# Token sums in two halves: reciprocals, stores and broadcasts of a recurrent attention loop

## The chip, the cores and the metric

The kernel runs on one core of one Trainium2 chip. The metric is the device time of one execution in microseconds. The reference is a plain array program; the kernel has to give its output from the same inputs in one launch. In the text PE is the matrix engine, DVE the vector engine, ACT the scalar engine, POOL the general engine, and SP the engine that issues nearly all transfers.

## The reference

Two branches read the same 2048 tokens of 512 channels and are mixed by a gate. The branch with the recurrence is what matters here:

```python
mem = mem0                                    # 8 rows of 512
for s in range(n_seg):                        # 64 segments of 32 tokens
    h = concatenate([mem, x[32 tokens]])      # 40 rows
    q, k, v = h @ Wq, h @ Wk, h @ Wv          # 32 heads of 128
    scores = where(mask, q @ k.T * scale, -1e9)
    o = softmax(scores) @ v
    o = einsum('bhte,hed->btd', o, Wo)
    mem = o[:, :8]                            # goes into the next segment
    outs.append(o[:, 8:])
out = g * concatenate(outs) + (1 - g) * mlp(layernorm(x))
```

The mask lets every row see the memory rows and lets a token see itself and what lies before it. A segment can't begin before the memory rows of the segment before it are there.

## The kernel before, in words

First comes the channel MLP of all tokens, from which a gated part `c` of the output goes to DRAM (`c_dr`) while the weights of the attention are loaded. After that a loop runs over the 64 segments; `T` is the tile of 128 tokens, `si` one of its four segments. The order of the instructions on every engine is written out by hand; the instructions of an engine, and the transfers that SP issues, run in the order of the program.

In a segment, 24 of the 32 tokens and the 8 memory rows are handled as one group of 32 rows; the 8 tokens that are left over in each of four segments ("left") are handled together for a whole tile. Work for the next tile's left rows (`side`) is put between the steps of a segment. The steps of a segment, in the order of PE:

- Q and K of the rows (`qk_unit`, line 124), copied by ACT (line 129) and transposed by DVE (line 133).
- Scores of the first sixteen heads into PSUM bank `SbF`, exponentials into `E` by ACT (line 751); V (line 143); then scores of the other sixteen into bank `W` (lines 294 and 298) and their exponentials (line 740).
- Sums over the keys. They are of two kinds. For the 8 memory rows `msum` gives the sums, and `mnorm` takes their reciprocal (line 747) and multiplies it into `E` (line 748), so these rows are normalized before the product with V. For the 32 tokens `xsums` (line 645) gives the sums of a half, 4 columns of `xs8`; the products with V are made with unnormalized `E`, and are normalized later.
- `recip_x` after the second half: one reciprocal of 8 columns (line 656), a store of it to DRAM (`r_dr`, line 659), and a load of it that is broadcast to all 128 partitions (`Rb`, 512 KB, line 660). The load waits until the store has landed.
- E V (`av`, lines 318 and 323), memory rows copied to `UT` (line 784), token rows to `XR` (line 651).
- The output pass (`wo_pass`, line 155) over `UT`, with the memory rows of this segment beside the tokens of the segment before; its memory rows go into the next segment through `new_mem` (lines 688 and 690).

The normalization of the tokens, `x_norm` on POOL (line 672), stands at the head of the next segment: `XR` times `Rb` into `UT` and `UL`. So a segment's tokens pass through the output pass of the segment after it. POOL also adds up the reciprocals (`racc`, line 664) and DVE keeps their minimum (`rmin`, line 804): at the end a flag is made from them, and if they are out of bounds a slow general version is run.

For all tiles but the last two, the outputs of the pass are four partial sums in partitions, which are brought together by DRAM: `put_w` (line 243) stores the output of a segment to `w_dr`, `get_w` (line 252) loads its four parts side by side into `G`, `put_left` (line 246) and `get_left` (four loads, line 256) do the same for the left rows, and `add_parts` (lines 261 to 269) adds them on DVE and stores the output. In the loop, before the change, these four stand at the head of a segment:

```python
        if s >= 2 and s - 2 < SPT * (NT - 2):
            put_w(s - 2, ws.pop(s - 2))
        if 4 <= s < SPT * (NT - 2) + 4:
            get_w(s - 4)
        if si == 3 and 1 <= T < NT - 1:
            put_left(T - 1)
        if si == 0 and T >= 2:
            get_left(T - 2)
```

Of the kernel before, what the change touches and what calls it, by code (L numbers as in the profile page):

```python
# [21 lines left out]
R_MIN = 1.0e-30  # L22
RSUM_MAX = 1.0e25
# [4 lines left out]
def kernel(ctx, tc, A_x, A_mem0, A_Wq, A_Wk, A_Wv, A_Wo, A_seg_len, B_x, B_w1, B_b1, B_w2, B_b2, gate_w, out):  # L28
    nc = tc.nc
    P = 128  # L30
# [210 lines left out]
    def put_w(s, w):  # L241
        T, si = divmod(s, SPT)
        nc.sync.dma_start(w_dr[T % 2][si], w[:])

    def put_left(T):
        nc.sync.dma_start(l_dr[T % 2][:], wls.pop(T)[:])

    def get_w(s):
        T, si = divmod(s, SPT)
        if si == 0:  # L250
            Gs[T] = cw.tile([P, 4, Dm], BF16, tag="G", name="G")
        nc.sync.dma_start(Gs[T][seg * si:seg * si + RIDE], w_dr[T % 2][si].rearrange("(c r) e -> r c e", c=4)[M:32])
# [76 lines left out]
    with tc.tile_pool(name="mlpw", bufs=1) as mlpw, \  # L329
# [44 lines left out]
        m0 = ep.tile([M, Dm], BF16)  # L374

        def loads(blk):
            if 2 * blk + 7 < NT:
# [270 lines left out]
    def x_raw(s):  # L648
# [2 lines left out]
            nc.scalar.copy(out=XR[:, j], in_=U[j][:, 0:NG * 40].rearrange("p (i q) -> p i q", q=40)[:, :, 0:32])  # L651
        XRs[s] = XR

    def recip_x(s):
        R = Rs.pop(s)
        nc.vector.reciprocal(out=R[:, 8 * NG:RW], in_=xs8)

        Rb = cw.tile([P, P, NG], FP32, tag="Rb", bufs=1, name="Rb")
        nc.sync.dma_start(r_dr[s % 2][:], R[:, 8 * NG:RW])
        nc.sync.dma_start(Rb[:].rearrange("p r e -> p (r e)"), r_dr[s % 2][:].rearrange("r e -> (r e)").partition_broadcast(P))  # L660
        for i2 in (1, 0):
            nc.vector.tensor_copy(out=R[:, 32 * i2:32 * i2 + 32], in_=RP[i2])
        mask_put(0)
        nc.gpsimd.tensor_tensor(out=racc[:, 0:RW], in0=racc[:, 0:RW], in1=R[:, 0:RW], op=ALU.add)  # L664
        Rbs[s] = Rb

    def x_norm(s):
        T, si = divmod(s, SPT)
        XR, Rb = XRs.pop(s), Rbs.pop(s)[:].rearrange("p (c q) (h j) -> p h j c q", c=4, h=2)
        for out, o, a, b in ((UT[(s + 1) % 2], M, LEFT, 32), (UL[T % 2], LEFT * si, 0, LEFT)):  # L670
            for h in range(2):
                nc.gpsimd.tensor_tensor(out=out[:, :, 4 * h:4 * h + 4, o:o + b - a], in0=XR[:, :, 4 * h:4 * h + 4, a:b], in1=Rb[:, h, :, :, a:b], op=ALU.mult)  # L672

    def wo_pass(U_, cuts=(0, Dm)):
        for n in range(NW):
# [18 lines left out]
    for s in range(nseg):  # L694
        T, si = divmod(s, SPT)
        last = s == nseg - 1
        hc, hn = hT[s % 3], hT[(s + 1) % 3]
        fill = side(T, si)
        if s + 1 < nseg:
            prep_h(s + 1)  # L700
        if s >= 1:
            x_norm(s - 1)
        if si == 0 and T >= 2:
            c_load(T - 2)
        if si < 3:
# [6 lines left out]
        if s >= 2 and s - 2 < SPT * (NT - 2):  # L712
            put_w(s - 2, ws.pop(s - 2))
        if 4 <= s < SPT * (NT - 2) + 4:
            get_w(s - 4)
        if si == 3 and 1 <= T < NT - 1:
            put_left(T - 1)
        if si == 0 and T >= 2:
            get_left(T - 2)
# [12 lines left out]
        V = cw.tile([P, NG, Dh], BF16, tag="V", name="V")  # L732
        E = cw.tile([P, NG, EW], BF16, tag="E", name="E")
        R = cw.tile([P, NG * 40], FP32, tag="R", name="R")
        Rs[s] = R
        xsum = SbF[:, 0:32 * NG].rearrange("p (i q) -> p i q", q=32)

        def exps(i2, x):
            c = slice(0, 40) if x else slice(40, EW)
            nc.scalar.activation(out=E[:, 4 * i2:4 * i2 + 4, c], in_=Sb[i2][:, :, c], func=ACTF.Exp, scale=scale)  # L740

        def msum(i2):
            sums(U[i2][:, 320:352].rearrange("p (i q) -> p i q", q=8), E[:, 4 * i2:4 * i2 + 4, :], 40, 48, 8, True)

        def mnorm(i2):
            r, e = RP[i2], E[:, 4 * i2:4 * i2 + 4, 40:56].rearrange("p i (a q) -> p i a q", q=8)
            nc.vector.reciprocal(out=r, in_=U[i2][:, 320:352])
            nc.vector.tensor_tensor(out=e, in0=e, in1=r.rearrange("p (i q) -> p i q", q=8).unsqueeze(2).to_broadcast([P, 4, 2, 8]), op=ALU.mult)

        scores(s, 0)  # L750
        nc.scalar.activation(out=E[:, 0:4, :], in_=Sb[0], func=ACTF.Exp, scale=scale)
        for kc in range(KC):
            v_unit(X1, hc, 0, kc)

        def v_cast(vb, h):
            i0 = 4 * vb + 2 * h
            nc.scalar.copy(out=V[:, i0:i0 + 2, :].rearrange("p i e -> p (i e)"), in_=(X1, X2)[vb][:, 256 * h:256 * h + 256])  # L757
# [48 lines left out]


    nx = slice(8 * NG, 40 * NG)
    sums(xsum, E, 8, 0, 32, True)
# [5 lines left out]
    nc.vector.reciprocal(out=R[:, nx], in_=SbF[:, 0:32 * NG])  # L815
    ws[s - 1] = wo_pass(UT[s % 2])
    Rr = R[:, nx].rearrange("p (i q) -> p i q", q=32)
# [7 lines left out]
    for _ in fill:  # L825
        pass
    flush(act_q, 9)
    nc.vector.tensor_tensor(out=rmin[:, nx], in0=rmin[:, nx], in1=R[:, nx], op=ALU.min)
    nc.vector.tensor_tensor(out=racc[:, nx], in0=racc[:, nx], in1=R[:, nx], op=ALU.add)
    okp = loop.enter_context(tc.tile_pool(name="okp", bufs=1))  # L830
    tot = okp.tile([P, 2], FP32)
    nc.vector.tensor_reduce(out=tot[:, 0:1], in_=rmin[:], axis=AX.X, op=ALU.min)
    nc.vector.tensor_reduce(out=tot[:, 1:2], in_=racc[:], axis=AX.X, op=ALU.add)
    good = okp.tile([P, 2], BF16)
    nc.vector.tensor_scalar(out=good[:, 0:1], in0=tot[:, 0:1], scalar1=R_MIN, scalar2=None, op0=ALU.is_gt)
    nc.vector.tensor_scalar(out=good[:, 1:2], in0=tot[:, 1:2], scalar1=RSUM_MAX, scalar2=None, op0=ALU.is_lt)
    wf = wo_pass(UF, (0, Dm // 2, Dm))

    wl, c = wls.pop(T), cs.pop(T)
# [140 lines left out]
```

## Time and profile before

| | us |
|---|---|
| median of 3 runs | 771.27 (769.58 to 772.21) |
| profiled execution | 773.18 |
| its span, first to last instruction | 771.4 |
| PE busy | 751.8 |
| ACT busy | 538.7 |
| DVE busy | 428.2 |
| POOL busy | 303.4 |

The mean granted clock of PE was 0.996. The profiled execution's own time is 1.8 us over its span, and 1.9 us over the median of the runs. An instruction group's row gives the line, the engine, the operation, what it writes and reads, the count, the busy time, the mean of one, and the idle time of the engine before it with what ended most of it. A timeline row gives start and duration in us from the span's start. Idle time of an engine that isn't the bottleneck costs nothing by itself.

### The profile page before, as it was taken

Reading aid. Unit: us, or ns where it says so; the run is one execution under the profiler, and the core shown is the slowest. Engines: PE = TensorE matmul, PEld = TensorE weight load, DVE = VectorE, ACT = ScalarE, POOL = GpSimd, SP = SyncE. Lnnn points to the kernel's source line nnn. Section 1 sums busy time; section 2 is a strip of 40 time slices with the busy share of each in tenths; the row PEclk is TensorE's granted clock in tenths of the full one; section 3 lists DMA queues with packets and bytes.
Section 4 is the critical chain, followed back from the end, with each engine's and each line's share of the span. In section 5 each row is a group of like instructions: output and inputs, shape, how many; then the busy total and the mean of one; then the engine's idle time right before and its main releaser. Section 6 shows DMA issues by size and latency. Waiting matters only on the chain.

```text
span 771.4 us, 43914 instructions
## 1 busy us (share of the span) xinstructions
PE 751.8 (97%) x19074; PEld 409.3 (53%) x19074; DVE 428.2 (56%) x1470; ACT 538.7 (70%) x1631; POOL 303.4 (39%) x522
## 2 busy tenths in 40 slices
PE   7999999999999999999999999999999999999996
PEld 5666555555455555555555555554555555555453
DVE  5776355544546455555646464645554564646454
ACT  4666677777677677777776777776777777777663
POOL 4111034342544443444435254544434443543441
PEclk9999999999999999999999999999999999999999
DMA  6779422323233433414333332332331333332312
GB/s 196 274 237 391 154 64 70 99 93 112 86 85 89 115 98 95 114 60 114 99 113 99 103 104 85 94 111 89 100 112 63 109 99 113 99 106 75 88 42 66
DMA packets 71688, 87.11 MB, mean 113 GB/s; under 512 B 23545, under 2 KB 61410, under 8 KB 69954
## 3 DMA queue, kind: packets, MB, share of 16 engines
q1 hardware_dynamic: 69762, 81.36, 34.0%
q8 instruction: 151, 2.47, 1.4%
q0 software_dynamic: 784, 1.97, 0.8%
q10 hardware_dynamic: 944, 0.92, 0.4%
q14 instruction: 47, 0.39, 0.2%
HBM read 64.30 MB, written 13.63 MB: 101 GB/s over the span
## 4 chain that ended last, share of the span: by engine, by line
PE 94%; DMA 2%; issue 1%; DVE 1%; ACT 1%; POOL 1%; DVEq 0%; POOLq 0%; SPq 0%; ACTq 0%
PE U L124 29%; PE X L143 18%; PE W L155 15%; PE X L124 7%; PE U L503 5%; PE U L318 4%; PE X L155 4%; PE SbF L497 2%; PE W L497 2%; PE U L305 1%; PE W L294 1%; PE U L688 1%; PE SbF L294 1%; PE SbF L645 1%; DMA b1r<-in_B_b_dram 1%
## 5 line engine op out<-in xcount | busy, mean ns | idle before, releaser
L672 POOL TENSOR_TENSOR UT<-XR,Rb 128x384 bf16<-128x384 bf16 x126 | 139.8, 1132 | 307.5 <-DMA Rb<-r_dr 254.8
L129 ACT CAST Tb<-U 128x512 bf16<-128x512 f32 x258 | 151.2, 586 | 80.2 <-PE U L124 79.8
L124 PEld LDWEIGHTS <-hT 128*32 128x32 bf16 x4096 | 103.5, 96 | 103.1 <-DVE hT L690 10.0
L143 PE MATMUL X<-Wv_sb,hT 128*32 128x512 bf16 x2048 | 144.1, 378 | 0.4 <-issue 0.4
L124 PE MATMUL U<-Wq_sb,hT 128*32 128x512 bf16 x2048 | 136.9, 381 | 0.4 <-DVE hT L690 0.4
L124 PE MATMUL U<-Wk_sb,hT 128*32 128x512 bf16 x2048 | 132.7, 379 | 0.0
L155 PE MATMUL W<-Wo_sb,UT 128*32 128x512 bf16 x2080 | 125.7, 380 | 1.9 <-ACT UT L784 0.8
L133 DVE STREAM_TRANSPOSE QT<-Tb 128x256 f32<-128x256 f32 x128 | 57.0, 446 | 81.8 <-ACT Tb L129 81.8
L757 ACT CAST V<-X 128x256 bf16<-128x256 f32 x256 | 88.7, 372 | 15.6 <-PE X L143 3.2
L690 DVE CAST hT<-U 128x8 bf16<-128x8 f32 x126 | 20.9, 167 | 132.4 <-PE U L688 125.0
L155 PEld LDWEIGHTS <-UT 128*32 128x32 bf16 x2080 | 56.4, 96 | 60.0 <-issue 16.5
L679 ACT CAST w<-W 128x128 bf16<-128x128 f32 (+1 forms) x192 | 46.0, 311 | 48.2 <-PE W L155 48.2
L651 ACT CAST XR<-U 128x256 bf16<-128x256 f32 x252 | 78.4, 434 | 0.0
L133 DVE STREAM_TRANSPOSE KT<-Tb 128x256 f32<-128x256 f32 x128 | 57.0, 445 | 28.1 <-ACT Tb L129 23.5
L672 POOL TENSOR_TENSOR UL<-XR,Rb 128x128 bf16<-128x128 bf16 x126 | 60.7, 506 | 0.0
L143 PEld LDWEIGHTS <-hT 128*32 128x32 bf16 x2048 | 46.5, 94 | 23.0 <-issue 2.4
L503 PE MATMUL U<-w_sb,hTm 128*128 128x512 bf16 (+1 forms) x176 | 52.5, 382 | 0.0
L784 ACT CAST UT<-U 128x64 bf16<-128x64 f32 x252 | 35.4, 226 | 23.2 <-PE U L323 23.2
L664 POOL TENSOR_TENSOR racc<-racc,R 128x72 f32<-128x72 f32 x63 | 22.7, 360 | 67.2 <-PE U L323 56.5
L740 ACT ACTIVATE E<-W 128x64 bf16<-128x64 f32 (+1 forms) x128 | 35.0, 273 | 15.7 <-PE W L298 14.8
L497 PEld LDWEIGHTS <-w_sb 128*128 128x128 bf16 (+1 forms) x352 | 34.6, 102 | 19.8 <-issue 1.3
L688 PEld LDWEIGHTS <-w 128*32 128x32 bf16 x1008 | 22.8, 93 | 36.7 <-ACT w L679 28.8
(160 smaller groups left out, 1249.5 us busy)
## 6 DMA issues: line engine op xcount, KB each, us to landing
Rb<-r_dr SPq DMA_DIRECT2D x63, 512.0 KB
w_dr<-w SPq DMA_DIRECT2D x56, 128.0 KB
G<-w_dr SPq DMA_DIRECT2D x56, 96.0 KB
Wv_sb<-in_A_Wv_dram SPq DMA_DIRECT2D x4, 1024.0 KB
Wq_sb<-in_A_Wq_dram SPq DMA_DIRECT2D x4, 1024.0 KB
Wk_sb<-in_A_Wk_dram SPq DMA_DIRECT2D x4, 1024.0 KB
Wo_sb<-in_A_Wo_dram SPq DMA_DIRECT2D x4, 1024.0 KB
VP<-VL SPq DMA_DIRECT2D x64, 64.0 KB
```

The costliest lines, as they stand in the source:

```text
L124: nc.tensor.matmul(bk[32 * j:32 * j + 32, :], lhsT=G[:, kc, :], rhs=W5[t][:, kc, h0:h1, j, :], start=(kc == 0), stop=(kc == KC - 1), tile_ ...
L129: nc.scalar.copy(out=Tb[:], in_=bk.rearrange("p (a b e) -> p a e b", a=8, b=2))
L133: nc.vector.transpose(out=dst[:, 8 * hf:8 * hf + 8, c0:c0 + 32, :].rearrange("p a r b -> p a (r b)").bitcast(FP32), in_=Tb[:].rearrange("p ...
L143: nc.tensor.matmul(bk[32 * j:32 * j + 32, :], lhsT=G[:, kc, :], rhs=Wv5[:, kc, 4 * vb:4 * vb + 4, j, :], start=(kc == 0), stop=(kc == KC - ...
L155: nc.tensor.matmul(bk[32 * c:32 * c + 32, :], lhsT=U_[:, j, i, :], rhs=Wo_sb[:, 4 * i + j, :], start=(n == 0), stop=(n == NW - 1), tile_po ...
L497: nc.tensor.matmul(hp[:rows, 0:TB * P], lhsT=w1_sb[:, kc, fc * P:fc * P + rows], rhs=yTs[blk][:, kc, :], start=(kc == 0), stop=(kc == KC - 1))
L503: nc.tensor.matmul(bp(blk, tt)[:], lhsT=hTm[blk % 2][:rows, fc, tt * P:(tt + 1) * P], rhs=w2_sb[:rows, fc, :], start=(fc == 0), stop=(fc = ...
L651: nc.scalar.copy(out=XR[:, j], in_=U[j][:, 0:NG * 40].rearrange("p (i q) -> p i q", q=40)[:, :, 0:32])
L672: nc.gpsimd.tensor_tensor(out=out[:, :, 4 * h:4 * h + 4, o:o + b - a], in0=XR[:, :, 4 * h:4 * h + 4, a:b], in1=Rb[:, h, :, :, a:b], op=ALU ...
L679: nc.scalar.copy(out=w[:, a:b], in_=W[:, a:b])
L757: nc.scalar.copy(out=V[:, i0:i0 + 2, :].rearrange("p i e -> p (i e)"), in_=(X1, X2)[vb][:, 256 * h:256 * h + 256])
L784: nc.scalar.copy(out=UT[s % 2][:, j, :, 0:M], in_=U[j][:, 0:NG * 40].rearrange("p (i q) -> p i q", q=40)[:, :, 32:40])
```

## The change

- The reciprocals of the token sums are taken in two halves of 4 columns (`recip_half`), into a buffer `RX` with room for all segments. The first half stands right behind the first half's sums, ahead of `mnorm(0)` on DVE; the second where the whole one stood. Each half has a store of its own.
- The broadcast becomes two loads, into two tiles of half the size, each with its own DRAM buffer; both stand behind the second store. The multiplications of `x_norm`, two halves before too, read one tile each.
- `put_w` and `get_w` go from the head of the segment to behind the first store; `put_left` and `get_left` to between the second store and the broadcasts.
- The running sum and minimum no longer hold the token sums (64 columns instead of 72); instead two reductions over `RX` stand behind the loop, and the last two comparisons take their results with a second scalar.
- `m0`, and `R` of the last segment, are allocated in other pools.

```diff
-    r_dr = [dram.tile([P, NG], FP32, name=f"r_dr{i}") for i in range(2)]
+    r_dr = [[dram.tile([P, NG // 2], FP32, name=f"r_dr{i}{h}") for h in range(2)] for i in range(2)]
...
+    RX = lp.tile([P, nseg - 1, NG], FP32)
...
-    RW = 9 * NG
+    RW = 8 * NG
...
+    def recip_half(s, h):
+        r = RX[:, s, 4 * h:4 * h + 4]
+        nc.vector.reciprocal(out=r, in_=xs8[:, 4 * h:4 * h + 4])
+        nc.sync.dma_start(r_dr[s % 2][h][:], r)
+
     def recip_x(s):
+        T, si = divmod(s, SPT)
+        recip_half(s, 1)
         R = Rs.pop(s)
-        nc.vector.reciprocal(out=R[:, 8 * NG:RW], in_=xs8)
-
-        Rb = cw.tile([P, P, NG], FP32, tag="Rb", bufs=1, name="Rb")
-        nc.sync.dma_start(r_dr[s % 2][:], R[:, 8 * NG:RW])
-        nc.sync.dma_start(Rb[:].rearrange("p r e -> p (r e)"), r_dr[s % 2][:].rearrange("r e -> (r e)").partition_broadcast(P))
+        if si == 3 and 1 <= T < NT - 1:
+            put_left(T - 1)
+        if si == 0 and T >= 2:
+            get_left(T - 2)
+        Rb = []
+        for h in range(2):
+            Rb.append(cw.tile([P, P, NG // 2], FP32, tag=f"Rb{h}", bufs=1, name="Rb"))
+            nc.sync.dma_start(Rb[h][:].rearrange("p r e -> p (r e)"), r_dr[s % 2][h][:].rearrange("r e -> (r e)").partition_broadcast(P))
...
-        XR, Rb = XRs.pop(s), Rbs.pop(s)[:].rearrange("p (c q) (h j) -> p h j c q", c=4, h=2)
+        XR, Rb = XRs.pop(s), [r[:].rearrange("p (c q) j -> p j c q", c=4) for r in Rbs.pop(s)]
...
             xsums(E, 0)
             msum(0)
+            recip_half(s, 0)
+            if s >= 2 and s - 2 < SPT * (NT - 2):
+                put_w(s - 2, ws.pop(s - 2))
+            if 4 <= s < SPT * (NT - 2) + 4:
+                get_w(s - 4)
             mnorm(0)
...
+    xr = RX[:].rearrange("p s e -> p (s e)")
+    nc.vector.tensor_reduce(out=tot[:, 0, 0:1], in_=xr, axis=AX.X, op=ALU.min)
+    nc.vector.tensor_reduce(out=tot[:, 1, 0:1], in_=xr, axis=AX.X, op=ALU.add)
```

More of the change, by code (lines that the diff above doesn't have):

```diff
@@ L373 @@
         ld_x(5)
-        m0 = ep.tile([M, Dm], BF16)
+        m0 = mlpw.tile([M, Dm], BF16)
         def loads(blk):
@@ L668, in x_norm @@
         T, si = divmod(s, SPT)
-        XR, Rb = XRs.pop(s), Rbs.pop(s)[:].rearrange("p (c q) (h j) -> p h j c q", c=4, h=2)
+        XR, Rb = XRs.pop(s), [r[:].rearrange("p (c q) j -> p j c q", c=4) for r in Rbs.pop(s)]
         for out, o, a, b in ((UT[(s + 1) % 2], M, LEFT, 32), (UL[T % 2], LEFT * si, 0, LEFT)):
             for h in range(2):
-                nc.gpsimd.tensor_tensor(out=out[:, :, 4 * h:4 * h + 4, o:o + b - a], in0=XR[:, :, 4 * h:4 * h + 4, a:b], in1=Rb[:, h, :, :, a:b], op=ALU.mult)
+                nc.gpsimd.tensor_tensor(out=out[:, :, 4 * h:4 * h + 4, o:o + b - a], in0=XR[:, :, 4 * h:4 * h + 4, a:b], in1=Rb[h][:, :, :, a:b], op=ALU.mult)
     def wo_pass(U_, cuts=(0, Dm)):
@@ L711 @@
             load_xT(T + 2)
[L712 to L719, printed above, removed]
         if si == 1 and T >= 2:
@@ L733 @@
         E = cw.tile([P, NG, EW], BF16, tag="E", name="E")
-        R = cw.tile([P, NG * 40], FP32, tag="R", name="R")
+        R = cw.tile([P, RW], FP32, tag="R", name="R")
         Rs[s] = R
@@ L808 @@
     nx = slice(8 * NG, 40 * NG)
+    okp = loop.enter_context(tc.tile_pool(name="okp", bufs=1))
+    R = okp.tile([P, 32 * NG], FP32)
+    tot = okp.tile([P, 2, 2], FP32)
+    xr = RX[:].rearrange("p s e -> p (s e)")
+    nc.vector.tensor_reduce(out=tot[:, 0, 0:1], in_=xr, axis=AX.X, op=ALU.min)
+    nc.vector.tensor_reduce(out=tot[:, 1, 0:1], in_=xr, axis=AX.X, op=ALU.add)
     sums(xsum, E, 8, 0, 32, True)
@@ L814 @@
     run(3)
-    nc.vector.reciprocal(out=R[:, nx], in_=SbF[:, 0:32 * NG])
+    nc.vector.reciprocal(out=R[:], in_=SbF[:, 0:32 * NG])
     ws[s - 1] = wo_pass(UT[s % 2])
-    Rr = R[:, nx].rearrange("p (i q) -> p i q", q=32)
+    Rr = R[:].rearrange("p (i q) -> p i q", q=32)
     nc.vector.tensor_tensor(out=E[:, :, 8:40], in0=E[:, :, 8:40], in1=Rr, op=ALU.mult)
@@ L827 @@
     flush(act_q, 9)
[L828 to L833, printed above, removed]
+    nc.vector.tensor_tensor(out=rmin[:, nx], in0=rmin[:, nx], in1=R[:], op=ALU.min)
+    nc.vector.tensor_tensor(out=racc[:, nx], in0=racc[:, nx], in1=R[:], op=ALU.add)
+    nc.vector.tensor_reduce(out=tot[:, 0, 1:2], in_=rmin[:], axis=AX.X, op=ALU.min)
+    nc.vector.tensor_reduce(out=tot[:, 1, 1:2], in_=racc[:], axis=AX.X, op=ALU.add)
     good = okp.tile([P, 2], BF16)
-    nc.vector.tensor_scalar(out=good[:, 0:1], in0=tot[:, 0:1], scalar1=R_MIN, scalar2=None, op0=ALU.is_gt)
-    nc.vector.tensor_scalar(out=good[:, 1:2], in0=tot[:, 1:2], scalar1=RSUM_MAX, scalar2=None, op0=ALU.is_lt)
+    nc.vector.tensor_scalar(out=good[:, 0:1], in0=tot[:, 0, 1:2], scalar1=tot[:, 0, 0:1], scalar2=R_MIN, op0=ALU.min, op1=ALU.is_gt)
+    nc.vector.tensor_scalar(out=good[:, 1:2], in0=tot[:, 1, 1:2], scalar1=tot[:, 1, 0:1], scalar2=RSUM_MAX, op0=ALU.add, op1=ALU.is_lt)
     wf = wo_pass(UF, (0, Dm // 2, Dm))
```

## The prediction

> **What bounds the kernel now.** I read the page first, then the waits, then single stretches of the timeline. From the page:
>
> ```profile
> span 771.4 us, 43914 instructions
> PE 751.8 (97%) x19074; PEld 409.3 (53%) x19074; DVE 428.2 (56%) x1470; ACT 538.7 (70%) x1631; POOL 303.4 (39%) x522
> q8 instruction: 151, 2.47, 1.4%
> PE 94%; DMA 2%; issue 1%; DVE 1%; ACT 1%; POOL 1%; DVEq 0%; POOLq 0%; SPq 0%; ACTq 0%
> L672 POOL TENSOR_TENSOR UT<-XR,Rb 128x384 bf16<-128x384 bf16 x126 | 139.8, 1132 | 307.5 <-DMA Rb<-r_dr 254.8
> ```
>
> PE is busy for 97% of the span and is 94% of the chain. The change works on the path from the token sums to POOL's products, and the waits put the largest number of the whole profile there:
>
> ```profile
> POOL UT L672 <- DMA Rb<-r_dr: 254.8, 52, 8.0
> SPq L660 <- DMA r_dr<-R: 102.5, 63, 2.9
> ```
>
> That number is a trap. POOL waits 254.8 us for the broadcast, but POOL is 1% of the chain: the products are wanted by the next segment's output pass only. If nothing else were in play, a broadcast that comes earlier would buy nothing. So the question is what PE loses inside the loop. The 128x8 reciprocal of the sums (line 656) stands once in every segment and is my clock; the first row is from the view by source line (duration least/median/most, then the first and the last start), the others from the timeline of two segments:
>
> ```profile
> L656 DVE RECIPROCAL R<-SbF x63: 201/208/210, 102.4 to 748.5; 128x8 f32<-128x8 f32 x63
> 446.60 0.21 DVE L656 RECIPROCAL R<-SbF 128x8 f32<-128x8 f32 x1
> 456.82 0.21 DVE L656 RECIPROCAL R<-SbF 128x8 f32<-128x8 f32 x1
> 185.36 0.20 DVE L656 RECIPROCAL R<-SbF 128x8 f32<-128x8 f32 x1
> 196.53 0.21 DVE L656 RECIPROCAL R<-SbF 128x8 f32<-128x8 f32 x1
> ```
>
> Sixty-two periods take 748.5 - 102.4 = 646.1 us, or 10.42 each. The undisturbed one here takes 10.22; of the 62 starts that the first row groups, half follow at 10.20 to 10.26, most at 10.23, and the one from 185.36 takes 11.17. At 10.23 throughout, the loop would last 634.3: **11.8 us are lost to irregular segments.** Where they go is seen on PE in the long one:
>
> ```profile
> 193.90 0.27 PE L294 MATMUL W<-QT,KT 128*32 128x40 bf16 x13
> 194.92 0.20 PE L294 MATMUL W<-QT,KT 128*32 128x40 bf16 x3 [0.75 <-issue]
> ```
>
> PE stops inside a group of sixteen like matmuls, after the thirteenth, and "issue" says that no semaphore holds it. The DMA view cut into short windows names the cause. The first row is 189.4 to 192.4, the second 192.4 to 192.5, the third 449.2 to 449.5, in an undisturbed segment:
>
> ```profile
> q1 hardware_dynamic: 497, 0.79, 88.6%
> q8 instruction: 1, 0.02, 62.9%
> q8 instruction: 1, 0.02, 21.1%
> ```
>
> The instruction queue moves 2.47 MB in 151 packets, 16 KB each. While the broadcast and what follows it kept the DMA engines 88.6% busy, no instruction packet ran; one began in the first tenth of a microsecond after the window. PE ran dry at about 194.2 and went on at 194.92. In the undisturbed segment the packet began just as that segment's broadcast did. So I read the lost 11.8 us as instruction packets held behind transfers, with the 512 KB broadcast the worst. When SP issues it:
>
> ```profile
> 185.82 0.61 SPq L659 DMA_DIRECT2D r_dr<-R  x1
> 188.47 0.34 SPq L660 DMA_DIRECT2D Rb<-r_dr  x1
> 188.90 0.55 SPq L184 DMA_DIRECT2D VP<-VL  x1
> 189.54 0.54 SPq L243 DMA_DIRECT2D w_dr<-w  x1
> 190.14 0.43 SPq L252 DMA_DIRECT2D G<-w_dr  x1
> 446.83 0.33 SPq L659 DMA_DIRECT2D r_dr<-R  x1
> 448.46 0.32 SPq L660 DMA_DIRECT2D Rb<-r_dr  x1
> 226.55 1.34 SPq L256 DMA_DIRECT2D G<-l_dr  x4
> ```
>
> On the loop's clock the store goes out 0.2 to 0.5 us after the reciprocal; the broadcast waits for it to land (1.6 us in the undisturbed case, 2.7 in the long one); and the partial outputs w_dr and G are queued right behind the broadcast, in the same train.
>
> [...]
>
> **The change part by part.** *The broadcast.* Now the first half's store leaves about 1.3 us before the second sums, and its landing is over when the second half's store is issued. The first broadcast (256 KB) then needs only its turn on SP: 0.24 + 0.33 after the reciprocal, so 0.6, where the whole one went out at 1.9 (448.46 - 446.60) or 3.1 (188.47 - 185.36). The second keeps the landing wait of the store, 1.6 us, so it goes out at about 1.9, with half the bytes. In the first segment of a tile the four loads of leftovers stand ahead of the broadcasts: 1.34 us of SP, which puts the first at 1.9 and the second right behind. The train of 3.0 us, seen from 189.4 to 192.4, shortens: 256 KB from 1.9 on is half of it, 1.5, so the last half ends about 1.2 to 1.5 us sooner, and between the halves an instruction packet may get in.
>
> *The partial outputs.* put_w and get_w go from the end of the train to between the two stores. They cost SP 0.54 + 0.43 there. The second store is issued behind both and may land later by their bytes (224 KB, at the 263 GB/s of the window 0.9 us at most). Nobody on PE waits for them: the sums of parts come a tile later.
>
> *What it is worth.* A packet freed 1.2 us earlier exceeds the 0.75 of the stop, and the 0.9 by which that segment is too long. So where the broadcast is the holder the stall goes. What share of the 11.8 that is the profile doesn't group: the ends are 0 (all stalls move elsewhere) and 11.8 (all go). I take half, **-6.0 us**, since packets can still be held by VP, w_dr, G and the output.
>
> *The added reciprocal.* DVE does 63 more instructions, ahead of the normalization of the memory rows. This is the place where the change can cost:
>
> ```profile
> 403.12 0.21 PE L645 MATMUL SbF<-BO,E 128*32 128x4 bf16 x8
> 403.20 0.19 PE L308 MATMUL U<-E,BO 128*32 128x32 bf16 x4
> 403.54 0.37 DVE L747 RECIPROCAL SbF<-U 128x32 f32<-128x32 f32 x1 [0.33 <-ACT V L757]
> 403.94 0.22 DVE L748 TENSOR_TENSOR E<-E,SbF 128x64 bf16<-128x64 bf16 x1
> 404.05 0.32 ACT L740 ACTIVATE E<-W 128x160 bf16<-128x160 f32 x1
> 404.40 0.37 DVE L747 RECIPROCAL W<-U 128x32 f32<-128x32 f32 x1 [0.24 <-ACT E L740]
> 404.80 0.22 DVE L748 TENSOR_TENSOR E<-E,W 128x64 bf16<-128x64 bf16 x1
> 405.08 0.29 PE L318 MATMUL U<-E,V 32*128 32x40 bf16 x16
> ```
>
> The second normalization ends at 405.02 and PE's second half of E V starts at 405.08: it is on the path. It starts at 404.40 because ACT's exponentials end at 404.37, after DVE idled 0.24. The half reciprocal (128x4; nearest row the 128x8 one, 0.208) begins between 403.48 (its sums end 0.06 before the others) and 403.54, so the first normalization ends between 404.31 and 404.37 instead of 404.16. Both fit the 0.24, by 0.03 to 0.09. Cost on the path 0; its upper bound is the 128x32 reciprocal's 0.37, of which 0.13 would stick out, 63 x 0.13 = 8.2 us. I take 0, since 128x4 lies near 128x8. A gain is excluded: nothing is taken from DVE there, and the later half costs what the whole did.
>
> *SP and the rest.* SP issues 126 more transfers of 0.33. What waits behind the first store's wait is put_w and get_w alone, for which nobody hurries. POOL's sum over 64 columns instead of 72 and the moved tiles cost nothing. Two reductions over 63 x 8 = 504 numbers come at the tail:
>
> ```profile
> 756.48 0.45 DVE L133 STREAM_TRANSPOSE KT<-Tb 128x256 f32<-128x256 f32 x1 [0.36 <-ACT Tb L129]
> 758.65 1.76 DVE L815 RECIPROCAL R<-SbF 128x256 f32<-128x256 f32 x1 [1.73 <-ACT V L757]
> L832 DVE TENSOR_REDUCE tot<-rmin 128x1 f32<-128x320 f32 x1 | 0.5, 478 | 0.0
> ```
>
> By elements one takes 0.478 x 504/320 = 0.75, two 1.5, within the 1.73 that DVE idles; uncovered, 1.5 us once. I take 0.
>
> **The sum.** -6.0 + 0 + 0 = -6.0. The profiled execution took 773.2 (span 771.4 and 1.8 around it), so 767.2; that execution lies 1.9 above the median of 771.27, and the same 6.0 takes the median to **765.3**.
>
> **The rivals.** *No change.* PE stays the bound and the stalls are only dealt out anew: the packets come at a fixed pace in the instruction stream, and a train that is moved meets others. For it: PE is busy for 97% already. Against: the train also shrinks, by half of 3.0 us for each part. It gives 771.3. [...] That the broadcast is not in truth earlier, because the second half still waits for a landing behind put_w and get_w (0.9 us), ends here too.
>
> *Slower by DVE.* The half reciprocal, with what it waits for, takes over 0.24 plus the 0.03 before the second normalization is late. From there every 0.1 us costs 6.3 us over 63 segments; at the bound of 0.13 it is +8.2, which is 779.5 without the gain and 773.5 with it. For it: the margin is 0.03 to 0.09. Against: rows of 201 to 210 ns for twice the elements.
>
> *More stalls.* The second store and the broadcasts meet instruction packets at new places, and as many again are held; half of 11.8 more gives 777.2.
>
> *Nearly all.* If every stall hangs on the broadcast, -11.8 gives 759.5.
>
> **How the numbers follow.** A gain, half or more: 0.64 (half 0.50, nearly all 0.14). No change: 0.14. Slower by DVE 0.14, by more stalls 0.08, together 0.22. About 0.3%, 2.3 us, is what a measurement can tell from no change; the three runs themselves lie 2.6 apart. The range goes from 759.5, all stalls gone, to 775.0, which takes in no change and the DVE bound with the gain, and leaves out slower cases without the gain, some 0.14. The likeliest case's own range is 760 to 769.
>
> **What would show it.** Right: broadcasts issued 0.6 and 1.9 after the second reciprocal, POOL's products begun about 1 us earlier in the segment, the normal period still 10.23, fewer stops by issue and 62 periods that last about 640 us. Wrong: a normal period over 10.23 with DVE's second normalization after 0.02 on the clock (the DVE rival), or the period kept and the sum of the 62 still at 646 (stalls only moved).

## The result, and the profile after

| | before | after |
|---|---|---|
| median of the runs, us | 771.37 (768.36 to 774.07, 20 runs) | 775.02 (770.89 to 779.64, 20 runs) |
| profiled execution, us | 773.18 | 776.42 |
| its span, us | 771.4 | 774.5 |
| 62 periods of the loop, us | 646.1 | 649.3 |

The ratio is 1.0047, with an interval of 1.0026 to 1.0067: the changed kernel is slower by 3.65 us, where 765.3 and a gain of 6 were forecast. Three later comparisons of the same kernel gave 0.9984 [0.9965, 1.0002], 1.0025 [1.0004, 1.0046] and 1.0022 [0.9997, 1.0046]; the mean of the four is 1.0020. So the loss is small, and the first comparison shows more of it than the others; but in none of the four is there a sign of the 0.8% that was forecast.

From the page of the changed kernel, the lines that answer to those of before, and the queue q1 that carries nearly all data:

```profile
span 774.5 us, 44134 instructions
PE 755.5 (98%) x19074; PEld 416.4 (54%) x19074; DVE 437.4 (56%) x1535; ACT 538.2 (69%) x1631; POOL 303.2 (39%) x522
...
q1 hardware_dynamic: 87906, 81.37, 40.2%
q8 instruction: 151, 2.47, 1.6%
...
PE 95%; DMA 1%; DVE 1%; issue 1%; ACT 1%; SPq 0%; DVEq 0%; ACTq 0%
...
L683 POOL TENSOR_TENSOR UT<-XR,Rb 128x384 bf16<-128x384 bf16 x126 | 141.3, 1129 | 300.8 <-DMA Rb<-r_dr 208.9
```

The same line for q1 on the page of the kernel before:

```profile
q1 hardware_dynamic: 69762, 81.36, 34.0%
```

Three things are to be read here. POOL waits 208.9 us for the broadcast, where it was 254.8: the largest wait of the profile became 46 us shorter, and the kernel did not become faster. PE is the bound as before. And the bytes of q1 are the same, 81.37 MB, in 18,144 more packets that take 40.2% of the DMA engines' time instead of 34.0%.

The loop itself lasts 751.83 - 102.50 = 649.3 us, from the second half's reciprocals (line 657; the timeline's first one and the view by source line, which ends with the last):

```profile
102.50 0.18 DVE L657 RECIPROCAL RX<-SbF 128x4 f32<-128x4 f32 x1
L657 DVE RECIPROCAL RX<-SbF x126: 173/182/184, 101.0 to 751.8; 128x4 f32<-128x4 f32 x126
```

Before and after the loop nothing changed: it begins at 102.50 instead of 102.42, and 22.6 us follow it instead of 22.9.

**The undisturbed period.** Over all segments the commonest period of this reciprocal is now 10.26, and it was 10.23. In these rows of the timeline one undisturbed segment shows where the 0.03 comes from, at the place that the prediction weighed (PE's sums, DVE and ACT up to E V):

```profile
666.39 0.18 PE L308 MATMUL U<-E,BO 128*32 128x32 bf16 x4
...
666.67 0.18 DVE L657 RECIPROCAL RX<-SbF 128x4 f32<-128x4 f32 x1 [0.28 <-PE U L308]
...
666.88 0.22 ACT L743 ACTIVATE E<-W 128x64 bf16<-128x64 f32 x1 [0.20 <-PE W L298]
...
666.95 0.36 DVE L750 RECIPROCAL SbF<-U 128x32 f32<-128x32 f32 x1
...
667.25 0.32 ACT L743 ACTIVATE E<-W 128x160 bf16<-128x160 f32 x1
667.35 0.22 DVE L751 TENSOR_TENSOR E<-E,SbF 128x64 bf16<-128x64 bf16 x1
...
667.61 0.37 DVE L750 RECIPROCAL W<-U 128x32 f32<-128x32 f32 x1
...
668.01 0.30 PE L318 MATMUL U<-E,V 32*128 32x40 bf16 x16
...
668.15 0.18 DVE L657 RECIPROCAL RX<-SbF 128x4 f32<-128x4 f32 x1
668.25 0.16 DVE L673 COPY R<-W 128x32 f32<-128x32 f32 x1
```

The half reciprocal ends at 666.85, and the first of ACT's two exponentials begins at 666.88. Over all segments of the loop that lag has a median of 0.033 us. The waits of ACT look as if it waited for the reciprocal; the first line is of the kernel before, the other two of the changed one:

```profile
ACT E L740 <- PE W L298: 14.8, 62, 1.3
```

```profile
ACT E L743 <- DVE RX L657: 10.0, 51, 0.2
...
ACT E L743 <- PE W L298: 3.3, 11, 1.0
```

Before, the list puts ACT's exponentials down to the scores in 62 of 63 segments; now it names the half reciprocal in 51. But ACT doesn't wait for it. The instruction has two semaphores to wait for, DVE's and PE's, and by the trace's semaphore events the wait for DVE was over in every segment at least 0.31 us before the half reciprocal began. What releases ACT, before the change and after it, is PE's signal that the scores are done: ACT begins 0.023 us behind it (median) in both kernels. In 55 of 63 segments this signal and that of the half reciprocal come within 0.002 us of each other, and the list decides such a tie by a nanosecond; the row at 666.88 above names PE. What the change moved is PE's signal itself. The last matmuls of the scores begin 0.17 us after the last sums over the memory rows (line 308) in both kernels, but the signal comes 0.46 after them instead of 0.44. Measured from the same sums, medians over the segments, ACT's first exponentials begin at 0.48 instead of 0.46, its second at 0.86 instead of 0.83, the second normalization on DVE at 1.21 instead of 1.19, and E V on PE at 1.61 instead of 1.58. On DVE too the room is used up: from the start of the half reciprocal to the start of the next instruction pass 0.28 us, not 0.18, since that instruction waits for the half reciprocal's own signal (the one behind the second half's, at 668.25 above, has no such wait and begins 0.10 after it). The second normalization's idle time ahead of it, all segments together, fell from 19.4 us to 5.2 (groups by line, the kernel before, then the changed one):

```profile
L747 DVE RECIPROCAL W<-U 128x32 f32<-128x32 f32 x63 | 23.1, 367 | 19.4 <-ACT E L740 18.6 <-PE X L143 0.7
```

```profile
L750 DVE RECIPROCAL W<-U 128x32 f32<-128x32 f32 x63 | 23.1, 366 | 5.2 <-PE X L143 1.6 <-PE U L308 0.9 <-ACT E L743 0.7
```

**The broadcasts.** SP's rows of the same segment of the changed kernel:

```profile
666.88 0.33 SPq L658 DMA_DIRECT2D r_dr<-RX  x1
667.26 0.42 SPq L243 DMA_DIRECT2D w_dr<-w  x1
667.73 0.40 SPq L252 DMA_DIRECT2D G<-w_dr  x1
668.37 0.32 SPq L658 DMA_DIRECT2D r_dr<-RX  x1
...
669.83 1.80 SPq L671 DMA_DIRECT2D Rb<-r_dr  x2
```

The second reciprocal stands at 668.15. The first broadcast goes out 1.68 us after it, not 0.6: the first store, issued at 666.88, is released as landed only 2.95 later. The second broadcast is the last 0.32 of the row, at 671.31, so 3.16 after the reciprocal, not 1.9. Over all segments the medians are 1.7 and 3.6 (before, the one broadcast had 2.0). The train did not shrink: the last packet of the broadcasts ends 7.2 us after the reciprocal (median; 6.7 to 7.2 in the four profiles of the changed kernel), where it ended at 6.1 before. POOL's products still begin earlier, 6.0 us after the reciprocal instead of 6.8, since the first half is there sooner. That sign of the prediction came true, and the gain did not come with it.

### The profile page after: what moved, and what is told of

The parts are those of the page before. It is cut to its first block, busy times and chain, and to the rows that moved or that the text cites. A ratio compares the mean times of both kernels' runs of the same rounds, so it can differ in the third digit from the quotient of the medians.

```text
span 774.5 us, 44134 instructions
## 1 busy us (share of the span) xinstructions
PE 755.5 (98%) x19074; PEld 416.4 (54%) x19074; DVE 437.4 (56%) x1535; ACT 538.2 (69%) x1631; POOL 303.2 (39%) x522
## 3 DMA queue, kind: packets, MB, share of 16 engines
q1 hardware_dynamic: 87906, 81.37, 40.2%
## 4 chain that ended last, share of the span: by engine, by line
PE 95%; DMA 1%; DVE 1%; issue 1%; ACT 1%; SPq 0%; DVEq 0%; ACTq 0%
PE U L124 30%; PE X L143 18%; PE W L155 15%; PE X L124 7%; PE U L503 4%; PE U L318 4%; PE X L155 4%; PE W L497 2%; PE SbF L497 2%; PE U L305 1%; PE W L294 1%; DMA w_sb<-in_B_w_dram 1%; PE U L699 1%; PE SbF L294 1%; PE SbF L646 1%
## 5 line engine op out<-in xcount | busy, mean ns | idle before, releaser
L683 POOL TENSOR_TENSOR UT<-XR,Rb 128x384 bf16<-128x384 bf16 x126 | 141.3, 1129 | 300.8 <-DMA Rb<-r_dr 208.9
L124 PEld LDWEIGHTS <-hT 128*32 128x32 bf16 x4096 | 105.7, 96 | 104.3 <-DVE hT L701 11.1
L143 PE MATMUL X<-Wv_sb,hT 128*32 128x512 bf16 x2048 | 146.4, 378 | 0.6 <-issue 0.6
L124 PE MATMUL U<-Wq_sb,hT 128*32 128x512 bf16 x2048 | 140.1, 381 | 0.7 <-DVE hT L701 0.4
L124 PE MATMUL U<-Wk_sb,hT 128*32 128x512 bf16 x2048 | 136.3, 379 | 0.2 <-issue 0.2
L683 POOL TENSOR_TENSOR UL<-XR,Rb 128x128 bf16<-128x128 bf16 x126 | 63.5, 527 | 0.0
L143 PEld LDWEIGHTS <-hT 128*32 128x32 bf16 x2048 | 50.9, 94 | 20.5 <-issue 1.6
L503 PE MATMUL U<-w_sb,hTm 128*128 128x512 bf16 (+1 forms) x176 | 52.5, 382 | 0.0
L675 POOL TENSOR_TENSOR racc<-racc,R 128x64 f32<-128x64 f32 x63 | 21.4, 340 | 76.7 <-PE U L323 64.2
```

The costliest lines, as they stand in the source:

```text
L124: nc.tensor.matmul(bk[32 * j:32 * j + 32, :], lhsT=G[:, kc, :], rhs=W5[t][:, kc, h0:h1, j, :], start=(kc == 0), stop=(kc == KC - 1), tile_ ...
L143: nc.tensor.matmul(bk[32 * j:32 * j + 32, :], lhsT=G[:, kc, :], rhs=Wv5[:, kc, 4 * vb:4 * vb + 4, j, :], start=(kc == 0), stop=(kc == KC - ...
L503: nc.tensor.matmul(bp(blk, tt)[:], lhsT=hTm[blk % 2][:rows, fc, tt * P:(tt + 1) * P], rhs=w2_sb[:rows, fc, :], start=(fc == 0), stop=(fc = ...
```

## The experiments

Each ratio is against the kernel before on the same chip in the same session, with its 95% interval; periods and spans are those of one profiled execution. The theory from the prediction's own rows was: instruction packets are held by the broadcast; the change moves the stalls about, and adds something. The rivals for what it adds were the half reciprocal, the moved transfers, and the split itself.

**The half reciprocal alone.** The kernel before, with one more reciprocal of the first half's sums; its result isn't used.

```diff
             msum(0)
+            nc.vector.reciprocal(out=rx0[:], in_=xs8[:, 0:4])
             mnorm(0)
```

> The kernel before, with one more DVE instruction a segment: a reciprocal of the first four columns of the token sums ahead of the first normalization, its result unused. No transfer differs. Theory DVE (the added reciprocal uses up the 0.24 us that DVE idled, and the second normalization comes later): the undisturbed period goes from 10.23 to 10.26 and the time up by 62 x 0.03 = 1.9 us, to 773.3. Theories of transfers (order, or the split): period 10.23, time 771.4, within 0.5.

Measured: 1.0015 [0.9993, 1.0037], and the period 10.26. So that one instruction makes the period of the changed kernel, with all else as before. 62 x 0.03 = 1.9 us, or 0.25%, is what the loop's clock gives; the timed ratio agrees but can't tell it from nothing.

**The same from the other side.** The changed kernel with the first half's reciprocal, its store and what SP issues behind it one step later.

```diff
             msum(0)
+            mnorm(0)
             recip_half(s, 0)
 ...
-            mnorm(0)
```

> The changed kernel with the first half's reciprocal behind the first normalization on DVE instead of ahead of it; all transfers in the same order. Theory DVE: period back to 10.23 and 1.9 us less than the changed kernel, 773.1. Theories order and split alone: as the changed kernel, 775, period 10.26.

Measured: 0.9970 [0.9948, 0.9992], span 762.8, period 10.23. Repeated beside the changed kernel on another chip:

> The changed kernel with the first half's reciprocal behind the first normalization, again, now beside the changed kernel. Theory DVE: 1.9 us (0.0025) below the changed kernel in any session. If putting the store and the held transfers 0.6 us later matters besides (0.997 beside 1.0047 before): 4 to 6 us below.

> The changed kernel, a third time. Two sessions gave 1.0047 and 0.9984. If the loss is 1.9 us by DVE in every run plus stalls that differ between sessions: 0.998 to 1.005, with periods at 10.26. If one of the sessions was an accident of that chip, this run repeats the other.

1.0006 [0.9987, 1.0024] for it and 1.0025 [1.0004, 1.0046] for the changed kernel as it stands, a difference of 1.7 us: about the 1.9. In both profiles of the late half the period is 10.23, and PE's signal comes 0.43 after the last sums again, ACT's exponentials at 0.46. Its second broadcast goes out later than in any other kernel (medians 3.9 and 4.1), and it isn't slower for that: how early the last broadcast goes out doesn't decide the time by itself.

**The moved transfers alone.** The kernel before, with put_w and get_w behind msum(0) and the left transfers between store and broadcast. No store stands ahead of put_w and get_w there, so in time only the left transfers move much.

```diff
         if si == 0 and T + 2 < NT:
             load_xT(T + 2)
-        if s >= 2 and s - 2 < SPT * (NT - 2):
-            put_w(s - 2, ws.pop(s - 2))
-        ...
             msum(0)
+            if s >= 2 and s - 2 < SPT * (NT - 2):
+                put_w(s - 2, ws.pop(s - 2))
+            ...
             mnorm(0)
```

> The kernel before with whole reciprocal, one store and one 512 KB broadcast, and only put_w and get_w moved to behind the first sums, put_left and get_left to between store and broadcast. Theory order (what stands ahead of the store keeps it from landing, so the last broadcast goes late and stalls stay): the store lands 2.5 to 3 us after its issue instead of 1.45, the broadcast goes out at 3 or later after the reciprocal instead of 1.7, time 772.5 to 774. Theory split (two broadcasts of 256 KB cost more than one of 512 KB): 771.4 or less. Theory DVE: 771.4, period 10.23.

Measured: 0.9969 [0.9951, 0.9988], a gain of 0.3%, where theory order had a loss. The other way round, the changed kernel with all four back at the head of the segment:

> The changed kernel with put_w, get_w, put_left and get_left back at the head of the segment: only the halves of the reciprocal, the two stores and the two broadcasts are left of the change. Theory order: second broadcast at about 1.8 after the second reciprocal instead of 3.4, the stalls of the changed kernel fewer, time 773 or less (of it 1.9 by DVE). Theory split: the broadcasts' packets still take about 130 us of 16 engines instead of 97, time 774 to 775. Theory DVE alone: 773.3, period 10.26.

1.0025 [1.0003, 1.0046]; its broadcasts go out at 0.6 and 1.9, as forecast, in the segments where nothing stands ahead of them (the third of a tile; over all segments the medians are 0.9 and 3.0). POOL's products begin 1.8 us earlier than in the kernel before (medians 5.0 and 6.8), and the kernel is not faster. So where the broadcasts did go out as forecast, the gain did not come with them. With only put_w and get_w at the head, and the changed kernel beside it:

> The changed kernel with put_w and get_w alone back at the head of the segment, where SP issues them as soon as it comes to them; put_left and get_left stay between the stores and the broadcasts, the halves stay. Theory held parts (put_w and get_w, held back by SP until the first half's reciprocal is there, run just ahead of the second store and the broadcasts, and that is what costs): ratio 0.998 to 1.001, made up of the moved left rows (0.997) and the added DVE instruction (1.002). Theory split (the two broadcasts cost): as the changed kernel, 1.004.

> The changed kernel once more, on the chip and beside the runs of the next three. If the loss belongs to the kernel, ratio 1.003 to 1.006 to the kernel before as the first time; a ratio within 0.002 of 1 would say that the loss hangs on the chip or on chance.

1.0017 [0.9999, 1.0035] and 0.9984 [0.9965, 1.0002]. So the moves are not what costs; if anything they give.

**Is the broadcast the holder?** The kernel before, with the broadcast in the first segment only; the later segments multiply by the first one's reciprocals, so the output is another.

```diff
-        nc.sync.dma_start(Rb[:]..., r_dr[s % 2][:]...partition_broadcast(P))
+        if s == 0:
+            nc.sync.dma_start(Rb[:]..., r_dr[s % 2][:]...partition_broadcast(P))
```

> The kernel before with the broadcast of the first segment only; all later segments multiply by that one (the stores of reciprocals stay, the output is not the reference's). Theory instruction packets (what the loop loses over 10.23 a segment hangs on the 512 KB broadcast): 4 to 10 us less than before, nearly all periods at 10.23. If the broadcast isn't the holder: within 2 us of before.

Measured: 0.9915 [0.9889, 0.9940], 6.5 us less. And with half the bytes, the reciprocals of the tokens in bf16 (they are left out of the flag's sum and minimum):

> The kernel before with the reciprocals of the token sums written, stored and broadcast in bf16 (256 KB instead of 512; these sums are left out of the final flag). Theory instruction packets: 2 to 5 us less than before, between before and the kernel without broadcast. If the broadcast isn't the holder: within 2 us.

0.9938 [0.9914, 0.9962], 4.3 us less, with one store and one broadcast as before. The same with the moves:

> The kernel before with the transfers moved as in the change and the reciprocals of the token sums in bf16 (256 KB broadcast; these sums left out of the final flag): the two edits that were each faster, 0.9969 and 0.9938. If their gains add: 0.991. If both remove the same stalls: 0.993 to 0.994.

0.9938 [0.9915, 0.9962]: once the broadcast is small, the moves bring nothing more. Of the 11.8 us that the loop loses to irregular segments, some 6.5 hang on the broadcast.

**The split of the broadcast.** The changed kernel with both stores into one buffer and one broadcast of 512 KB, which waits for both; the early half stays.

```diff
-        for h in range(2):
-            Rb.append(cw.tile([P, P, NG // 2], ...))
-            nc.sync.dma_start(Rb[h][:]..., r_dr[s % 2][h][:]...partition_broadcast(P))
+        Rb = cw.tile([P, P, NG], ...)
+        nc.sync.dma_start(Rb[:]..., r_dr[s % 2][:]...partition_broadcast(P))
```

> The changed kernel with both halves stored into one DRAM buffer and one broadcast of 512 KB behind the second store: everything else, the order of the transfers and the early reciprocal too, as in the changed kernel. Theory split (two broadcasts of 2 KB rows cost the engines more than one of 4 KB rows): broadcast packets at 97 instead of 131 us of 16 engines, 2 to 4 us below the changed kernel. Theory order: the broadcast still goes out 3 after the reciprocal, time as the changed kernel within 1.5.

Measured: 0.9983 [0.9965, 1.0002], 3.4 us under the changed kernel of the same session. From its page, and from that of the changed kernel in the same session:

```profile
q1 hardware_dynamic: 78834, 81.37, 35.9%
```

```profile
q1 hardware_dynamic: 87906, 81.37, 39.0%
```

The two stores are in both, so the difference is that of the split: 0.390 x 772.6 - 0.359 x 767.4 = 25.8 us of all sixteen engines for the same bytes. The other profiles of the changed kernel have 38.2 to 40.2%, so one pair of profiles gives the size only roughly. The broadcasts' own packets in the loop say it more directly: 8,064 of 4 KB with a mean of 0.20 us, 102 us of sixteen engines in all, against 16,128 of 2 KB with a mean of 0.12 to 0.14 us, 124 to 136 us in the four profiles of the changed kernel. That is 22 to 34 us more, 0.35 to 0.54 in each segment. This kernel's single broadcast goes out at 3.0 after the reciprocal (median), later than the 2.0 of the kernel before, and it is the faster one for all that. Then the split alone, in the kernel before, with nothing moved (one reciprocal, two stores, two broadcasts), and a copy of the kernel before beside it:

> The kernel before with its one reciprocal of 8 columns, then two stores of halves and two broadcasts of 256 KB right behind each other; no other transfer moved, DVE as before. Theory split: broadcast packets take 120 to 131 us of 16 engines instead of 97, ratio 1.002 to 1.005, period 10.23. If the split costs nothing by itself: ratio within 0.0015 of 1.

> The kernel before, unchanged, as if it were an edit. Its ratio to itself shows what two series of one kernel differ by: within 0.001 of 1 if the sessions differ only by chance between executions; 0.002 or more if each series has stalls of its own.

1.0141 [1.0091, 1.0191] for the split and 1.0006 [0.9982, 1.0031] for the copy. The split, with the second store that belongs to it, makes the kernel slower by 12.3 us (784.65 against 772.37); in the profile its 62 periods take 660.5 us instead of 646.1. It is not a fixed price, though. The kernel above with all four transfers back at the head has the same split and the same order of transfers, and differs by the early half (and by where the reciprocals are kept): it is at 1.0025, with its broadcasts at 0.9 and 3.0 instead of 2.4 and 3.2 (medians). In the kernel with the split alone, the longest of PE's waits that no semaphore explains:

```profile
PE SbF L645 <- issue: 3.0, 2, 1.6
PE X L143 <- issue: 2.6, 6, 1.0
PE W L294 <- issue: 2.0, 4, 0.8
PE U L318 <- issue: 1.9, 4, 0.9
```

One of these waits, with the DMA view of the 3.0 us before it (455.2 to 458.2) and of the tenth after (458.2 to 458.3), is the picture of the prediction again, longer:

```profile
453.59 1.89 SPq L663 DMA_DIRECT2D Rb<-r_dr  x2
455.53 0.54 SPq L184 DMA_DIRECT2D VP<-VL  x1
456.16 0.54 SPq L243 DMA_DIRECT2D w_dr<-w  x1
456.75 0.44 SPq L252 DMA_DIRECT2D G<-w_dr  x1
459.20 0.39 PE L143 MATMUL X<-Wv_sb,hT 128*32 128x512 bf16 x4
460.59 1.05 PE L143 MATMUL X<-Wv_sb,hT 128*32 128x512 bf16 x16 [1.00 <-issue]
```

```profile
q1 hardware_dynamic: 340, 0.51, 80.3%
```

```profile
q8 instruction: 1, 0.02, 57.8%
```

For 3.0 us no instruction packet ran while q1 kept the engines 80.3% busy with 0.51 MB; in the kernel before a window of the same length moved 0.79 MB at 88.6%. The packet came when the train was over, and PE stood still for a microsecond in the middle of V. The packet was done at 459.17, and PE went on 1.42 us later. That lag is regular: in the loop of the kernel before, in all ten stops without a semaphore of over 0.25 us, PE went on 1.2 to 1.8 us after the end of the last instruction packet, and in all 21 of this kernel 1.2 to 1.6 after it. So these stops do hang on the packets.

**The change without its two costs.** One broadcast, and the first half behind mnorm(0); the changed kernel for a fourth time beside it.

> The changed kernel with one broadcast of 512 KB, and the first half's reciprocal behind the first normalization: both named costs taken out, the moved transfers kept. Theories DVE and split together: 4 to 6 us below the changed kernel, ratio 0.995 to 0.998 to the kernel before. If one of the two were wrong: 2 to 3.5 us below.

> The changed kernel, a fourth time, beside the others. 1.001 to 1.005 if the sessions scatter about 1.9 us by DVE and some stalls; the mean of all four says whether the change is slower.

0.9945 [0.9919, 0.9970] and 1.0022 [0.9997, 1.0046]. This version is 5.5 us faster than the kernel before and 6.8 faster than the changed one, with the moved transfers and the two stores kept. Its broadcast goes out at 3.4 after the reciprocal (median) and its last packet ends at 7.1, both later than before: it is not an earlier broadcast that makes it faster.

## Why the prediction was wrong

All that PE waited without a semaphore, summed over the rows of that kind in the waits of PE (the whole span), puts the kernels side by side. "Over 10.23" is what 62 periods last beyond 62 x 10.23. The middle columns are of one profiled execution each, which lies up to 3.5 us from the median of its kernel's runs; the ratio is of the medians.

| kernel | PE idle by issue, us | period | over 10.23, us | ratio |
|---|---|---|---|---|
| before, and its copy | 5.9, 6.0 | 10.23 | 11.8, 12.9 | 1, 1.0006 |
| changed, four profiles | 4.9, 3.7, 3.6, 3.9 | 10.26 | 15.1, 9.9, 12.3, 12.8 | 1.0047, 0.9984, 1.0025, 1.0022 |
| half reciprocal alone | 3.3 | 10.26 | 7.3 | 1.0015 |
| split alone | 14.5 | 10.23 | 26.3 | 1.0141 |
| moves alone | 2.8 | 10.23 | 6.5 | 0.9969 |
| changed, all four at the head | 1.7 | 10.26 | 5.8 | 1.0025 |
| changed, put_w and get_w at the head | 3.7 | 10.26 | 11.1 | 1.0017 |
| changed, late half, two profiles | 0.6, 3.9 | 10.23 | 3.1, 9.1 | 0.9970, 1.0006 |
| one broadcast | 0.7 | 10.26 | 7.1 | 0.9983 |
| one broadcast, late half | 0.8 | 10.23 | 4.6 | 0.9945 |
| bf16 | 0 | 10.23 | 2.5 | 0.9938 |
| bf16 and moves | 0.4 | 10.23 | 3.8 | 0.9938 |
| no broadcast | 0.3 | 10.23 | 2.7 | 0.9915 |

*What bounds the kernel: right in the main.* PE is the bound, POOL's 254.8 us were a trap, and PE does stop for instruction packets that the broadcast holds. Without the broadcast, or with half of it, these stops are gone (0.3 and 0 us), and 4.3 to 6.5 us with them. But only 5.9 of the 11.8 us stand in the table's column of idle time. PE's busy time for the same 19,074 matmuls differs too: 751.8 us before, 755.5 in the first profile of the changed kernel; the 747.4 without the broadcast lack 13 matmul records of line 503, some 3.0 us (49.5 for 163 of them, 52.5 for 176 before). The rows of matmuls overlap (on line 143, 2,048 rows of 0.38 us in 144.1 us of busy time), so that a short stop needn't show as idle; that the rest of the loss sits there is argued, not shown. By the idle column alone the changed kernel would be the better one, 3.6 to 4.9 us against 5.9. In the kernel before, the packets come at a fixed pace in the instruction stream, as the rival "no change" has it, only on average: 151 packets to 43,914 recorded instructions, 291 each, but in the loop 172 to 413 from the start of one packet to that of the next.

*The broadcast, 0.6 and 1.9 us after the reciprocal: wrong.* This step took it that the first store's landing is over when the second is issued, and that the second keeps its 1.6 of landing. Both stores, of 2 KB, had company: put_w and get_w (224 KB) were now issued right behind the first, and the second stood behind them and beside the first broadcast. In the segment shown the first was released 2.95 us after its issue; over all segments the second broadcast went out at 3.6 (median) instead of 1.9. That the company is the reason is shown in the third segment of a tile, where nothing else stands ahead: with put_w and get_w back at the head the second broadcast goes out there at 1.8, in the changed kernel at 3.2, and the first at 0.6 and 0.7. The prediction had this delay (0.9 us at most) among the things that nobody waits for, and again in the rival "no change"; the second broadcast waits for it, and it is larger.

*The train ends 1.2 to 1.5 us sooner, worth -6.0: the step that failed.* It priced half the bytes at half the time, and half of the whole train at that: the 3.0 us moved 0.79 MB, of which half a broadcast is a third. And it took the second half to go out no later than the whole had. Instead the split made the same bytes dearer, by 22 to 34 us of all sixteen engines (0.35 to 0.54 a segment), and the last packet ended 0.6 to 1.0 us later than before, not 1.2 to 1.5 sooner. Alone in the kernel before it takes PE's stops from 6 us to 14.5. In the changed kernel it costs less than there: 1.0025 against 0.9983 in one session, and 0.9988 (mean of the two late halves) against 0.9945 across sessions, so 0.42 to 0.43% or 3.3 us both times, each with an uncertainty of some 0.3%. A train's end isn't the whole price either: the last version above ends its train at 7.1 and is the fastest of those that broadcast 512 KB in every segment. The packets of the broadcasts took 0.20 us for 4 KB and 0.12 to 0.14 for 2 KB, so two of 2 KB took 22 to 34% more. Whether the shorter packets are dearer by themselves, or wait more beside other packets, the packet times don't tell.

*The added reciprocal, cost 0: wrong, and small.* The margin was reckoned on DVE alone, 0.24 of idle against a reciprocal of about 0.2. On DVE 0.28 pass; since it begins 0.05 sooner than the normalization did, that leaves next to nothing of the 0.24. The step left out that the work beside it could become later too: PE's signal of the scores, and with it ACT's exponentials, for which the second normalization waits, come 0.02 to 0.03 later. It comes to 0.03 a segment, 1.9 us: every profile with the early half has a period of 10.26, every one without it 10.23, so that the instruction is the cause is shown, the way from it to PE's signal is not. The rival "slower by DVE" had the place right and put too much on it (8.2 at its bound).

*The partial outputs and the tail: right, with one reservation.* The moves by themselves gain 0.3%. The two reductions cost 0.64 and 0.66 (0.75 forecast) and lie in the idle time of the reciprocal behind them, which fell from 1.73 to 0.49:

```profile
760.24 0.64 DVE L821 TENSOR_REDUCE tot<-RX 128x1 f32<-128x504 f32 x1
760.80 0.66 DVE L822 TENSOR_REDUCE tot<-RX 128x1 f32<-128x504 f32 x1
761.95 1.76 DVE L829 RECIPROCAL R<-SbF 128x256 f32<-128x256 f32 x1 [0.49 <-PE SbF L308]
```

**The sum as it came out.** All the rest of the change -0.55% (one broadcast, late half), the split +0.43%, the early half +0.25% by the clock: +0.13%, against +0.20% as the mean of four comparisons. The first two terms together are just the mean of the late halves, and each term has an interval of about 0.2%, so the sign of so small a sum is not sure from it alone. That the rest gains 5.5 us, near the forecast's 6.0, is chance: the forecast put its gain on an earlier and smaller last broadcast, and the kernel with that gain has one of 512 KB that goes out later. The moved transfers, which the prediction took to be worth nothing to PE, give 0.3% of it by themselves; where the rest of it comes from wasn't tried.

**What stays open.** Why the changed kernel's four ratios lie 0.6% apart, with the same instructions, when a copy of the kernel before differs by 0.06% in its one session: the stalls over 10.26 in its four profiles go from 8.0 to 13.2 us, but what deals them out so differently was not found. Why the split costs three times as much in the unmoved kernel, and next to nothing beyond the half reciprocal there once the first store leaves early, is open: w_dr and G follow the broadcasts in both, so the order of the transfers isn't the reason. And the trace doesn't say why PE's signal of the scores comes 0.02 us later when the half reciprocal runs beside them.

## What to carry to other kernels

Splitting this broadcast into two halves did not leave what it takes the same: with packets of 2 KB instead of 4 KB the same bytes took 124 to 136 us of sixteen engines in the loop instead of 102. Look at packets and the queue's share for the same bytes before counting on an earlier half. A small store that gates something did not land sooner for standing ahead of large transfers: here 2 KB were released after 2.95 us with 224 KB right behind them, where 4 KB with nothing behind took 1.6. Price its landing with what is issued right behind it. An instruction put into an idle gap of one engine is to be checked by the period and by what the engines beside it do, not only against the gap: a reciprocal of 0.18 us in a gap of 0.24 took the period from 10.23 to 10.26. And when a list of waits names a new releaser, look whether another signal came in the same nanoseconds before believing it: here two came within 0.002 us of each other in 55 of 63 segments.

## What the runs showed of the hardware

- The packets of a broadcast took 0.20 us each on average at 4 KB a row and 0.12 to 0.14 at 2 KB a row in two broadcasts (one broadcast, and the four profiles of the changed kernel); the 81.37 MB of q1 took 275.5 us of sixteen engines with the first and 301.3 with the second in one session (35.9% of 767.4 and 39.0% of 772.6).
- A 4 KB store was released as landed 1.6 us after its issue with no transfer behind it (446.83 in the kernel before), and one of 2 KB 2.95 us after it with 224 KB behind it (666.88 in the changed one).
- PE stopped beside 16 KB instruction packets that came late: in the split kernel one began between 458.2 and 458.3 and was done at 459.17, and PE, dry at 459.59, went on at 460.59. In the loops of the kernel before and of the split one all 10 and all 21 stops without a semaphore of over 0.25 us ended 1.2 to 1.8 us after the end of an instruction packet. With the broadcast gone, all that PE waited without a semaphore fell from 5.9 us to 0.3 in the whole span.
- A reciprocal of 128x4 took 0.18 us by its row. DVE's next instruction began 0.28 after its start where it waits for the reciprocal's signal, and 0.10 after it where it doesn't.
- PE's signal that the scores are done came 0.44 us after the last sums before, and 0.46 with a 128x4 reciprocal on DVE beside the scores, though PE's last matmuls of them began at the same 0.17.
